# Keys and values of batches 1 to 7 loaded through GpSimd's queue in place of SP's, in a fused kernel of pooled attention and two expert layers

## Chip, cores and metric

One core of a Trainium2 chip. The metric is the device time of one execution in microseconds (us), the median of several runs. All times below are us unless marked ns.

## What is computed

```python
def _attn_ref(q, k, v):                       # (8, 8, 576, 64) each, f32
    k_p = k.reshape(B, H, Sp, pool, D).mean(axis=3)      # pool = 8, Sp = 72
    v_p = v.reshape(B, H, Sp, pool, D).mean(axis=3)
    scores = scale * np.matmul(q, k_p.transpose(0, 1, 3, 2))
    scores = scores - np.max(scores, axis=-1, keepdims=True)
    attn = np.exp(scores)
    attn = attn / (np.sum(attn, axis=-1, keepdims=True) + 1e-09)
    return np.matmul(attn, v_p)
...
x = ...                                       # (4608, 512): the heads side by side
x = g1(x @ w_in) @ w_out                      # 512 -> 2048 -> 512, g1 a clipped square
return g2(x @ w2_in) @ w2_out                 # the same sizes, g2 = relu squared
```

The keys and values of a batch are thus averaged over 8 neighbouring rows before the attention uses them. A batch has 8 heads, and the kernel takes them in pairs: four loads of keys and four of values per batch, `("k", b, p)` and `("v", b, p)` with p = 0 to 3, 64 pairs in all.

## The kernel before

The program is one long row of matmuls on TensorE. The tokens go through in tiles of 128 rows (36 tiles, in blocks of 4), and a loop over steps issues, for each step, the 12 matmuls of the first expert layer's input product (`ph`, L714: hi and lo halves of the operands, three products), one slot of attention work, the 12 matmuls of its output product (`acc`, L775 and L786), and a second slot of attention work. So the attention of a later tile runs between the matmuls of an earlier block. In the last 620 us or so only the second expert layer is left (`cp`, `dp` and their like, L1072 and L1081).

ScalarE (ACT) and VectorE (DVE) work beside it: they split operands into hi and lo (`wihi`/`wilo`, `wohi`/`wolo` at L237 and L241, `gh`/`gl` at L749 and L755), apply the activation (`g`, L747), make the softmax, transpose the attention weights (`aT`, L517, the operand of `px`, L529), and prepare the weights of the second layer (`cb`, L193, out of `z`, L165 to L219). GpSimd (POOL) has few instructions: it clears small pads (L965), and adds integer words for the weights of the second layer (L182); each such add waits for a piece that DVE made (L174), and DVE or ACT go on with its result.

Keys and values come like this. `load_kv` (L292 to L319) takes a buffer of the pool `kvp`, tag `kv`, which has three buffers, and starts the DMA from DRAM. For batches 0 and 1 the pair is laid out over 128 partitions and takes two DMAs (L303, 256 KB, and L313, 32 KB; in batch 0 L309 loads the second part for all pairs at once), and TensorE sums the rows itself (`unit_k` L346, `unit_v` L367), straight out of the loaded buffer. For batches 2 to 7 a load is one DMA of 288 KB over 72 partitions (L317), and `pool_kv` makes the sums on DVE: two adds in place (L332) and a third (L333) that writes `kp` or `vp`. After the third add the buffer is free. `pool_to` (L594 to L600) fixes the order in the program: pair n is summed, and right behind it the load of a later pair is issued. When each pair is due is set by the table `pool_at` (L577).

The program's order is not the engines' order. A scheduler of the tile framework takes the instructions and sets the order on each engine from its own costs, dependencies and buffers. Each engine and each engine's DMA queue then runs strictly in the order set. Before the change SP issues every DMA of the kernel but one or two, 1451 in all: weights, queries, the stores of the attention weights to DRAM and back (`pd<-pad`, L659, and `z<-pd`, L513), results, and the keys and values.

Of the kernel before, what the change touches and what calls it, by code (L numbers as in the profile page):

```python
# [34 lines left out]
def pooled_attention_moe_moe(  # L35
# [11 lines left out]
    nc = tc.nc  # L47
# [244 lines left out]
    def load_kv(nm, b, p):  # L292
        if b == 0 and p == NP - 1:

            a = cv.tile([P, 2, POOL * D], F32, tag="st", name="kv")
        else:
            a = kvp.tile([P if b < ON_PE else SP, 2, POOL * D], F32, tag="kv", name="kv")
        src = k if nm == "k" else v
        kv_t[nm, b, p] = a
        if b < ON_PE:  # L300

            src = src[b, 2 * p:2 * p + 2]
            nc.sync.dma_start(  # L303
                out=a[:, :, 0:BY * D], in_=src[:, 0:BY * P, :].rearrange("h (s r) d -> s h (r d)", r=BY)
            )
            if b == 0:
                if p == (1 if nm == "k" else 0):
                    rest[nm] = gp.tile([S - BY * P, H, D], F32, tag="gh", name="rest")
                    nc.sync.dma_start(  # L309
                        out=rest[nm], in_=(k if nm == "k" else v)[b, :, BY * P:S, :].rearrange("h s d -> s h d")  # L310
                    )
                return
            nc.sync.dma_start(  # L313
                out=a[0:S - BY * P, :, BY * D:(BY + 1) * D], in_=src[:, BY * P:S, :].rearrange("h s d -> s h d")
            )
            return
        nc.sync.dma_start(  # L317
            out=a, in_=src[b, 2 * p:2 * p + 2].rearrange("h (s r) d -> s h (r d)", r=POOL)
        )  # L319

# [235 lines left out]
    for t in range(TB0, NTILE):  # L556
# [12 lines left out]
        if t in first_tile:  # L569
            b = first_tile.index(t)  # L570
# [19 lines left out]
    def load_kv_to(n):  # L590
        while kv_loaded[0] < min(n, len(kv_order)):
            load_kv(*kv_order[kv_loaded[0]])
            kv_loaded[0] += 1
# [604 lines left out]
    for n, u in enumerate(units):  # L1198
        kind, b, i, g = u
# [56 lines left out]
```

## Time and profile before

| | us |
|---|---|
| median of 3 runs | 1620.85 (1620.62 to 1620.98) |
| the profiled execution, its own time | 1620.48 |
| its span in the profile | 1618.7 |
| TensorE (PE) busy | 1612.0 (100%) |
| VectorE (DVE) busy | 1246.5 (77%) |
| ScalarE (ACT) busy | 905.0 (56%) |
| GpSimd (POOL) busy | 54.1 (3%) |
| granted clock of TensorE | 1.00 in every stretch |

How to read it: the span is what the profile sees of the program on the core; the execution's own time is 1.8 longer and is what the runs are compared by. Busy times are sums over instructions; issuing a DMA is not counted as busy. The median stands 0.4 above the profiled execution.

### The profile page before, as it was taken

The numbers are of one execution on the slowest core, as the hardware profiler recorded it, in microseconds if no ns is written. First come the engines' busy times: TensorE is split into PE (matmuls) and PEld (weight loads), VectorE is DVE, ScalarE is ACT, GpSimd is POOL, SyncE is SP. The second block draws the span as 40 slices with busy tenths as digits, with TensorE's granted clock in tenths as the row PEclk, the third lists the DMA queues.
The fourth block names the chain that finished last, engine by engine and source line by source line (L and its number), as shares of the span: only waits on it lengthen the run. The fifth ranks groups of instructions, "written<-read, shape, count | busy, mean of one in ns | idle before, by whom it ended". The sixth has DMA issues, their size and how long they took to land.

```text
span 1618.7 us, 23331 instructions
## 1 busy us (share of the span) xinstructions
PE 1612.0 (100%) x7866; PEld 1317.1 (81%) x7866; DVE 1246.5 (77%) x2231; ACT 905.0 (56%) x1676; POOL 54.1 (3%) x60
## 2 busy tenths in 40 slices
PE   9999999999999999999999999999999999999998
PEld 7678888888878888888888888888888888888887
DVE  6999889898898999998975542578558855975585
ACT  7786566666666666666775532345335533553353
POOL 0000000100000000010100000000000000000000
PEclk9999999999999999999999999999999999999999
DMA  9753344554454554543560474566776776758565
GB/s 257 233 176 99 96 127 151 167 163 120 133 157 147 170 146 132 170 136 134 183 220 7 133 264 148 193 218 207 200 251 220 217 229 210 222 184 252 194 206 142
DMA packets 250279, 283.91 MB, mean 175 GB/s; under 512 B 123440, under 2 KB 155824, under 8 KB 250160
## 3 DMA queue, kind: packets, MB, share of 16 engines
q1 hardware_dynamic: 249072, 282.16, 56.5%
q8 instruction: 63, 1.03, 0.3%
q14 instruction: 56, 0.46, 0.1%
q10 hardware_dynamic: 1088, 0.26, 0.1%
HBM read 217.71 MB, written 64.62 MB: 174 GB/s over the span
## 4 chain that ended last, share of the span: by engine, by line
PE 98%; DMA 1%; DVE 1%; SPq 0%; issue 0%; ACT 0%; DVEq 0%; ACTq 0%
PE ph L714 27%; PE acc L786 26%; PE cp L1072 11%; PE dp L1081 10%; PE dq L1081 5%; PE cr L1072 5%; PE dr L1081 3%; PE cq L1072 3%; PE pss L411 2%; PE px L529 2%; PE acc L775 1%; PE pv L367 0%; DMA kv<-in_v_dram 0%; DMA w<-w2i 0%; PE pk L346 0%; PE dp L1182 0%
## 5 line engine op out<-in xcount | busy, mean ns | idle before, releaser
L714 PE MATMUL ph<-xhi,wihi 128*128 128x512 f32 x576 | 229.9, 399 | 0.0
L1029 ACT ACTIVATE gh<-g 128x512 fp32r<-128x512 f32 x224 | 139.9, 630 | 152.9 <-DVE g L1098 47.9
L714 PE MATMUL ph<-xlo,wihi 128*128 128x512 f32 x576 | 225.0, 391 | 0.0
L714 PE MATMUL ph<-xhi,wilo 128*128 128x512 f32 x576 | 224.9, 390 | 0.0
L786 PE MATMUL acc<-gh,wohi 128*128 128x512 f32 x552 | 222.6, 403 | 0.0
L786 PE MATMUL acc<-gl,wohi 128*128 128x512 f32 x552 | 216.1, 391 | 0.0
L786 PE MATMUL acc<-gh,wolo 128*128 128x512 f32 x552 | 215.5, 390 | 0.0
L821 DVE TENSOR_TENSOR gl<-g,gh 128x512 fp32r<-128x512 f32 x224 | 151.9, 689 | 49.7 <-ACT gh L1029 48.2
L1072 PE MATMUL cp<-x,w 128*128 128x512 f32 x768 | 186.4, 390 | 0.2 <-DMA w<-w2i 0.2
L1072 PEld LDWEIGHTS cp<-x,w 128*128 128x128 f32 x768 | 143.9, 188 | 31.5 <-ACT s L1094 1.4
L237 ACT ACTIVATE wihi<-wi 128x512 fp32r<-128x512 f32 x144 | 90.6, 629 | 123.4 <-PE ph L714 122.7
L1081 PE MATMUL dp<-gh,w 128*128 128x512 f32 x496 | 156.8, 390 | 0.0
L241 DVE TENSOR_TENSOR wilo<-wi,wihi 128x512 fp32r<-128x512 f32 x144 | 101.9, 708 | 46.5 <-ACT wihi L237 43.5
L714 PEld LDWEIGHTS ph<-xhi,wihi 128*128 128x128 f32 x576 | 108.1, 188 | 26.7 <-issue 3.8
L714 PEld LDWEIGHTS ph<-xhi,wilo 128*128 128x128 f32 x576 | 108.2, 188 | 23.1 <-issue 0.2
L714 PEld LDWEIGHTS ph<-xlo,wihi 128*128 128x128 f32 x576 | 108.3, 188 | 21.1 <-issue 0.2
L755 DVE TENSOR_TENSOR gl<-g,gh 128x512 fp32r<-128x512 f32 x154 | 107.0, 695 | 23.1 <-ACT gh L749 20.4
L749 ACT ACTIVATE gh<-g 128x512 fp32r<-128x512 f32 x138 | 86.8, 629 | 64.4 <-DVE g L747 63.5
L1094 ACT ACTIVATE s<-cp 128x512 f32<-128x512 f32 x96 | 57.1, 595 | 116.8 <-PE cp L1072 116.0
L786 PEld LDWEIGHTS acc<-gl,wohi 128*128 128x128 f32 x552 | 103.7, 188 | 22.9
L786 PEld LDWEIGHTS acc<-gh,wohi 128*128 128x128 f32 x552 | 103.8, 188 | 20.9 <-issue 0.6
L786 PEld LDWEIGHTS acc<-gh,wolo 128*128 128x128 f32 x552 | 103.9, 188 | 19.9
(161 smaller groups left out, 2953.3 us busy)
## 6 DMA issues: line engine op xcount, KB each, us to landing
w<-w2i SPq DMA_DIRECT2D x224, 256.0 KB
w<-w2o SPq DMA_DIRECT2D x224, 256.0 KB
w2i<-cb SPq DMA_DIRECT2D x32, 512.0 KB
w2o<-cb SPq DMA_DIRECT2D x32, 512.0 KB
st<-in_moe_w_in_dram SPq DMA_DIRECT2D x30, 512.0 KB
st<-in_moe_w_out_dram SPq DMA_DIRECT2D x30, 512.0 KB
pd<-pad SPq DMA_DIRECT2D x31, 384.0 KB
z<-pd SPq DMA_DIRECT2D x93, 128.0 KB
```

Of the source, the lines that this page charges most:

```text
L237: nc.scalar.activation(out=hi, in_=src, func=AF.Copy)
L241: eng.tensor_tensor(out=lo, in0=src, in1=hi.bitcast(F32), op=ALU.subtract)
L411: nc.tensor.matmul(out=pss[off:off + n, i, :], lhsT=qT[t][:, p, off:off + n], rhs=kbd[b % 2][:, p, :], start=True, stop=True,)
L714: nc.tensor.matmul(out=ph, lhsT=a[:, kk % a.shape[1], :], rhs=c[:, kk, :], start=(i == 0), stop=(i == 3 * KD - 1))
L749: act(out=gh, in_=g, func=AF.Copy)
L755: nc.vector.tensor_tensor(out=gl, in0=g, in1=gh.bitcast(F32), op=ALU.subtract)
L786: nc.tensor.matmul(out=o, lhsT=lhsT, rhs=rhs, start=(f == 0 and x == 0), stop=(f == KF - 1 and x == 2),)
L821: tt(out=out, in0=a, in1=b, op=ALU.subtract)
L1029: act(out=hi, in_=a, func=AF.Copy)
L1072: nc.tensor.matmul(out=out[0], lhsT=w[:, a, k, :], rhs=xq[b, i][c][:, k, :], start=(n == 0 and i in (1, 2, 7)), stop=(n == 5), skip_group_ ...
L1081: nc.tensor.matmul(out=out[d], lhsT=w[:, a, d, :], rhs=x[c], start=(g == 0 and n == 0 and i in (1, 2, 7, 4)), stop=(g == NG - 1 and n == 2 ...
L1094: act(out=snaps[key], in_=a, func=AF.Copy)
```

## The change

`load_kv` gets a variable `queue`, which is SP's queue for batch 0 and GpSimd's for batches 1 to 7, and issues its four DMA calls on it:

```diff
         src = k if nm == "k" else v
+        queue = nc.sync if b == 0 else nc.gpsimd
         kv_t[nm, b, p] = a
         if b < ON_PE:
 
             src = src[b, 2 * p:2 * p + 2]
-            nc.sync.dma_start(
+            queue.dma_start(
                 out=a[:, :, 0:BY * D], in_=src[:, 0:BY * P, :].rearrange("h (s r) d -> s h (r d)", r=BY)
             )
...
-            nc.sync.dma_start(
+            queue.dma_start(
                 out=a[0:S - BY * P, :, BY * D:(BY + 1) * D], in_=src[:, BY * P:S, :].rearrange("h s d -> s h d")
             )
             return
-        nc.sync.dma_start(
+        queue.dma_start(
             out=a, in_=src[b, 2 * p:2 * p + 2].rearrange("h (s r) d -> s h (r d)", r=POOL)
         )
```

64 DMAs move: 16 of batch 1 (eight pairs, two DMAs each) and 48 of batches 2 to 7. SP keeps 1387. From L299 on, every line of the changed kernel has a number higher by one: L303, L313, L317, L332, L333 become L304, L314, L318, L333, L334.

The scheduler answers with another order on several engines. Numbers behind a name count tiles as they are made; `kv_4796` is the same pair before and after.

**GpSimd, the stretch of batches 4 and 5.** Before, its queue holds nothing but the adds of L182 there:

```order
L182 TENSOR_TENSOR z<-st,z 128x512 x2
L182 TENSOR_TENSOR z<-st 128x4x2x32 x4
```

After, the loads stand among these adds, and each waits for a DVE instruction (the one that frees its buffer):

```order
L318 DMA kv_4276<-in_v_dram 72x2x512 [waits DMASW4_49,DVE_49]
L318 DMA kv_4355<-in_k_dram 72x2x512 [waits DMASW5_49,DVE_49]
L318 DMA kv_4664<-in_k_dram 72x2x512 [waits DMASW6_49,DVE_49]
L318 DMA kv_4727<-in_k_dram 72x2x512 [waits DMASW7_49,DVE_49]
L182 TENSOR_TENSOR z_3698<-st_3631,z_3698 128x512 [waits DMAHW1_49,DVE_49,Activation_49]
L182 TENSOR_TENSOR z_3977<-st_3975 128x4x2x32 [waits DVE_49,DMAHW1_49,Activation_49,Pool_49]
L182 TENSOR_TENSOR z_3977<-st_3975 128x4x2x32
L182 TENSOR_TENSOR z_4179<-st_4119 128x4x2x32 [waits DMAHW7_49,DVE_49,Activation_49]
L182 TENSOR_TENSOR z_4179<-st_4119 128x4x2x32
L318 DMA kv_4796<-in_k_dram 72x2x512 [waits DMASW0_49,DVE_49]
L318 DMA kv_4892<-in_v_dram 72x2x512 [waits DMASW1_49,DVE_49]
```

The order of the loads among themselves is that of the program; what is new is that they and the adds of L182 stand in one queue. With three buffers, `kv_4796` takes the buffer that `kv_4355` had.

**VectorE, where the keys of batch 5 are summed.** Before, the stretch from the sum of `kv_4664` to the first add of `kv_4727`:

```order
L333 TENSOR_TENSOR kp_4723<-kv_4664 72x128 [waits DVE_49]
L217 TENSOR_TENSOR s12_4705<-s12_4705,z_4448 128x256 [waits DVE_49]
L241 TENSOR_TENSOR wolo_4620<-wo10_1286,wohi_4619 128x512 [waits Activation_49]
L755 TENSOR_TENSOR gl_4565<-g_4566,gh_4564 128x512 [waits Activation_49]
L218 TENSOR_TENSOR z_4448<-z_4448,z_4636 128x256 [waits DVE_49]
L219 TENSOR_TENSOR z_4448<-z_4448,s12_4705 128x256
L193 TENSOR_TENSOR cb_4775<-s12_4705,cb_4775 128x2x256 [waits Activation_49]
L241 TENSOR_TENSOR wilo_4630<-wi12_1176,wihi_4629 128x512 [waits PE_49,Activation_49]
L332 TENSOR_TENSOR kv_4727<-kv_4727 72x2x256 [waits DMAHW4_49]
```

After, the stretch from the add that frees `kv_4355`'s buffer to the first add of `kv_4796`, which was loaded into that buffer:

```order
L334 TENSOR_TENSOR kp_4660<-kv_4355 72x128 [waits PE_49]
L334 TENSOR_TENSOR kp_4723<-kv_4664 72x128 [waits PE_49]
L748 SCALAR_TENSOR_TENSOR g_4104<-ph_4063,u_4105 128x512 [waits Activation_49]
L193 TENSOR_TENSOR cb_4390<-z_3977,cb_4390 128x2x256 [waits DMAHW3_49,Activation_49]
L334 TENSOR_TENSOR kp_4792<-kv_4727 72x128 [waits PE_49]
L756 TENSOR_TENSOR gl_4103<-g_4104,gh_4102 128x512 [waits Activation_49]
L241 TENSOR_TENSOR wolo_4158<-wo2_675,wohi_4157 128x512 [waits Activation_49]
L333 TENSOR_TENSOR kv_4796<-kv_4796 72x2x256 [waits DMASW3_49]
```

Between the release and the first add that needs the new load stand six instructions. The sums stand earlier in the program than before (their neighbours belong to earlier steps: `g_4104` after, `g_4566` before).

**TensorE, the first expert step after the first block.** The unit of keys of batch 1 whose second pair is `kv_605`. Before:

```order
L346 MATMUL pk_635<-pad1_122,kv_172 64x64 x8
L346 MATMUL pk_635<-pad1_122,kv_172 64x8 x2
L714 MATMUL ph_686<-xhi_415,wihi_570 128x512
L714 MATMUL ph_686<-xlo_416,wihi_570 128x512
L714 MATMUL ph_686<-xhi_415,wilo_571 128x512
L714 MATMUL ph_686<-xhi_415,wihi_570 128x512
L714 MATMUL ph_686<-xlo_416,wihi_570 128x512
L714 MATMUL ph_686<-xhi_415,wilo_571 128x512
L714 MATMUL ph_686<-xhi_415,wihi_570 128x512
L714 MATMUL ph_686<-xlo_416,wihi_570 128x512
L714 MATMUL ph_686<-xhi_415,wilo_571 128x512
```

After:

```order
L715 MATMUL ph_686<-xhi_415,wihi_570 128x512
L715 MATMUL ph_686<-xlo_416,wihi_570 128x512
L715 MATMUL ph_686<-xhi_415,wilo_571 128x512
L715 MATMUL ph_686<-xhi_415,wihi_570 128x512
L715 MATMUL ph_686<-xlo_416,wihi_570 128x512
L715 MATMUL ph_686<-xhi_415,wilo_571 128x512
L715 MATMUL ph_686<-xhi_415,wihi_570 128x512
L347 MATMUL pk_635<-pad1_122,kv_605 64x64 x8
L347 MATMUL pk_635<-pad1_122,kv_605 64x8 x2
```

The keys' matmuls now stand behind seven matmuls of `ph` and not behind eleven. Elsewhere TensorE's order changes in one other place only.

## Rows read from the trace of the kernel before

**Rows 1.** The page, part 1: busy time, share and instructions of each engine.

```profile
PE 1612.0 (100%) x7866; PEld 1317.1 (81%) x7866; DVE 1246.5 (77%) x2231; ACT 905.0 (56%) x1676; POOL 54.1 (3%) x60
```

**Rows 2.** The page, part 4: the chain that ended last, by engine.

```profile
PE 98%; DMA 1%; DVE 1%; SPq 0%; issue 0%; ACT 0%; DVEq 0%; ACTq 0%
```

**Rows 3.** Stretches: busy PE, PEld, DVE, ACT, POOL; clock, DMA share, GB/s.

```profile
40.00:100.00 60.00, 59.90 (x340) 40.27 (x340) 56.19 (x106) 46.81 (x113) 0.26 (x1) 1.00 0.72 213
...
400.00:500.00 100.00, 100.00 (x531) 81.31 (x530) 90.28 (x174) 63.87 (x117) 8.33 (x7) 1.00 0.46 139
```

**Rows 4.** Costliest groups by shape, L332 and L182: busy, mean ns, idle before.

```profile
L332 DVE TENSOR_TENSOR kv<-kv 72x512 f32<-72x512 f32 x48 | 34.8, 726 | 0.0
...
L182 POOL TENSOR_TENSOR z<-st,z 128x512 int32<-128x512 int32 x16 | 26.0, 1626 | 383.4 <-DVE z L174 159.9 <-ACT u L738 60.8 <-ACT u L737 58.3
...
L332 DVE TENSOR_TENSOR kv<-kv 72x256 f32<-72x256 f32 x48 | 19.8, 415 | 0.1
```

**Rows 5.** The timeline of SP's queue, three stretches: start, us, instruction.

```profile
42.32 0.38 SPq L303 DMA_DIRECT2D kv<-in_k_dram  x1
42.75 0.61 SPq L313 DMA_DIRECT2D kv<-in_k_dram  x1
...
166.03 0.34 SPq L659 DMA_DIRECT2D pd<-pad  x1
...
168.46 1.32 SPq L513 DMA_DIRECT2D z<-pd  x3
...
388.81 1.34 SPq L317 DMA_DIRECT2D kv<-in_k_dram  x3
```

**Rows 6.** The timeline of DVE, 405 to 419.

```profile
407.73 0.28 DVE L333 TENSOR_TENSOR kp<-kv 72x128 f32<-72x128 f32 x1
407.93 0.42 DVE L217 TENSOR_TENSOR s<-s,z 128x256 f32<-128x256 f32 x1
408.27 0.68 DVE L241 TENSOR_TENSOR wolo<-wo,wohi 128x512 fp32r<-128x512 f32 x1
408.87 0.68 DVE L755 TENSOR_TENSOR gl<-g,gh 128x512 fp32r<-128x512 f32 x1
...
411.35 0.68 DVE L332 TENSOR_TENSOR kv<-kv 72x512 f32<-72x512 f32 x1
...
418.07 1.23 DVE L517 STREAM_TRANSPOSE aT<-z 96x1024 f32<-96x1024 f32 x1
```

**Rows 7.** The chain of waits followed through 15 to 140: start, us, what.

```profile
43.94 2.74 PE ph L714 x11
...
61.50 1.30 DVE wo L174 x2
63.65 6.36 DMA kv<-in_v_dram
```

**Rows 8.** The chain of waits followed through 0 to 12.

```profile
4.52 4.67 DMA q<-in_q_dram
```

**Rows 9.** The timeline of PE, 41 to 50.

```profile
46.61 0.90 PE L346 MATMUL pk<-pad,kv 128*64 128x64 f32 x20
```

**Rows 10.** The timeline of weight loads, 69 to 71; idle before in brackets.

```profile
69.52 0.20 PEld L367 LDWEIGHTS pv<-kv,pad 64*72 64x72 f32 x2 [0.16 <-DMA kv<-in_v_dram]
70.05 0.86 PEld L367 LDWEIGHTS pv<-kv,pad 128*72 128x72 f32 x8 [0.33 <-DMA kv<-in_v_dram]
```

**Rows 11.** The timeline of PE, 414 to 426.

```profile
415.56 0.40 PE L786 MATMUL acc<-gl,wohi 128*128 128x512 f32 x1
...
423.93 1.09 PE L529 MATMUL px<-aT,vp 72*64 72x128 f32 x16
```

**Rows 12.** What SP's queue waited for: us in total, times, longest.

```profile
SPq L303 <- PE pk L346: 12.1, 2, 11.0
```

**Rows 13.** Costliest groups by shape, L168 and L174.

```profile
L168 DVE TENSOR_SCALAR z<-z 128x512 uint32<-128x512 uint32 x32 | 13.5, 422 | 0.6
...
L174 DVE SCALAR_TENSOR_TENSOR st<-st,z 128x512 uint32<-128x512 uint32 x16 | 11.0, 688 | 0.2
```

More of the change, by code (lines that the diff above doesn't have):

```diff
@@ L316, in load_kv @@
             return
-        nc.sync.dma_start(
+        queue.dma_start(
             out=a, in_=src[b, 2 * p:2 * p + 2].rearrange("h (s r) d -> s h (r d)", r=POOL)
```

## The prediction

> **What bounds the kernel now.** I read the page's busy times first. TensorE is busy for 1612.0 of the span's 1618.7 us [rows 1], so 6.7 us is all that any faster supply could give back, and most of that lies at the program's start and end. The chain that ended last says the same from the other side: 98% of it is TensorE, and 1% each is a DMA and VectorE [rows 2]. Then the stretches: from 100 us on TensorE has no idle time, while DVE is busy for 90.28 of 100 us between 400 and 500 [rows 3]. The reader should see two things there. DVE is the one helper with little to spare, about 9.7 us per 100. And a change of the kernel's time can come only from making TensorE wait, or from a wait that it already has. The groups of L332, 48 adds of either shape, had waited 0.0 and 0.1 us in all [rows 4], so DVE never waited for keys or values. The timelines say why: SP issued three loads at 388.81 [rows 5], and the first add of the second of them ran at 411.35 [rows 6], 22 us later. That lead hides whatever a load takes.
>
> **The change, part by part.** 64 DMAs leave SP's queue. For SP that is 64 issues of some 0.4 us [rows 5], off the path, and for the DMA engines the same bytes.
>
> What costs is the order that comes with it. The loads now stand in one queue with GpSimd's adds, and DVE's sums stand earlier. In the piece of DVE's order shown with the change, six instructions lie between the add that frees a buffer and the first add on what is loaded into it: two of `kp` and four of full size. On DVE's timeline a `kp` takes 0.20 from its start to the next start (407.73 to 407.93) and a full one 0.60 (408.27 to 408.87) [rows 6]: 2 × 0.20 + 4 × 0.60 = **2.8 us of cover**, where before it was 22. I counted the same cover over the whole order for the 45 loads whose buffer DVE frees: 2.8 at six of them (of `kv_3726`, `kv_4276`, `kv_4796`, `kv_6163`, `kv_6696`, `kv_7232`), 2.9, 3.3 and 3.5 at three more, 4.1 at three, 4.5 to 5.1 at seven, and more than that at the others.
>
> Against the cover stands L, the time from a buffer's release to the landing of the load that GpSimd issues into it. The trace of before has no such DMA, so I bound it. From below: a store of 384 KB was issued at 166.03, and its reader's DMAs went out at 168.46, 2.43 later [rows 5]. From above: a load of values, on the chain at 63.65, took 6.36, in a stretch with the DMA engines at a share of 0.72 [rows 7, 3]. Between them, a 256 KB read of queries took 4.67 [rows 8]. A load here reads 288 KB from DRAM, as that one does, but with the DMA share at 0.46 [rows 3] and not in the rush of the start, so somewhat less. GpSimd's part in issuing is not in the trace; SP's issue was 0.34 to 0.61 [rows 5], one GpSimd add 1.63 [rows 4], and I take 1.0 within the total. **L = 4.5**, bounds 2.4 and 6.4.
>
> The Trainium skill, DMA: Bandwidth & Descriptors, section "Anatomy of one DMA — SWDGE (gpsimd) path", gives 2.0 us plus the bytes over 436e3 for one DMA issued from GpSimd; an estimate from that page for 288 KB is 2.7 us, just under the smallest cover, and the sum by it would be about no change. No run here shows such a DMA yet.
>
> Another DVE fact may bear on L. The same 128x512 shape takes 422 ns in L168 and 688 in L174 [rows 13], so some DVE instructions run in a faster mode here. The Trainium skill, SBUF — State Buffer, section "SBUF: two separate sides", says that while DVE runs in such a mode GpSimd cannot write its descriptors. By that rule up to one instruction, 0.4 us, would be added to L where one of them meets an issue; the sum would grow by about 1 us. No row here shows it.
>
> The terms:
>
> 1. *Keys of batch 1 on TensorE.* SP's load of the last pair was issued at 42.32 and 42.75 [rows 5], when its buffer had come free, and TensorE reached it at 46.61 [rows 9] without waiting. Eleven matmuls before it took 2.74, so 0.25 each [rows 7]; it now stands four earlier, at about 45.7. Cover 3.4, two DMAs by GpSimd, the second some 0.2 behind: 4.5 + 0.2 − 3.4 = **+1.3** (0 with L under 3.2; 4.0 with L = 6.4 and 1.0 more for the second issue).
> 2. *Values of batch 1.* TensorE's two waits for a load before 70.05 were 0.16 and 0.33 [rows 10]: SP issued it behind loads that waited for DVE (61.50 to 62.80) [rows 7]. On GpSimd it waits for its buffer only: **−0.5** (0 to −0.5).
> 3. *DVE's waits.* Six at 4.5 − 2.8 = 1.7 are 10.2. Those at 2.9 to 3.5 add 1.6 + 1.2 + 1.0, those at 4.1 three times 0.4: 15.2, and about 12 once loads that stand right behind a wait are counted as partly paid by it. What TensorE feels of it is less. A `gl` that ended at 409.55 was used at 415.56, 6.0 later, and an `aT` that ended at 419.30 was used at 423.93, 4.6 later [rows 6, 11]; one wait of 1.7 is within that, and DVE's 9.7 idle us per 100 win it back in 18 us. Only waits that stand close together reach TensorE. I take a quarter: **+2.8**. The lower bound is 0, if each finds its slack. The upper one is L = 6.4: six at 3.6, three at 3.2, three at 2.3 and seven at 1.6 are 49 us of waits, about all of DVE's idle time from 100 to 700 (58 by the row of 400 to 500), of which I let 20 through.
> 4. *ACT and SP near the seventh tile* (130 us) run in another order, with two splits of weights ahead of the evacuation of a transpose: **+1.0** (0 to 2, the time of three such splits).
>
> Sum: 1.3 − 0.5 + 2.8 + 1.0 = +4.6. Against the profiled execution's 1620.48 that gives 1625.1; the median stands 0.4 above the profiled one, so **1625.4** on the scale of 1620.85. A measurement of this kernel can tell about 0.2% from no change, which is 3.2 us.
>
> **The rivals.**
>
> *A, the forecast:* slower by 3.3 to 11 us, because L is over the smallest covers. Chance 0.44.
>
> *C, landing inside the cover: no change.* The place is the first add after a release; the price is the difference L − 2.8; it decides at L of about 3.3, where six waits of 0.5 vanish in slacks of 4.6 and 6.0, term 1 is near 0, and terms 2 and 4 cancel. Time about 1621. For it speaks the store's 2.43 and that SP's load from 42.75 landed before 46.61, within 3.9 at a DMA share of 0.72. Against it speaks the 4.67 of the queries, and that GpSimd's issue is one more step. It also covers the case that L is 4 and all waits are absorbed. Chance 0.39. The figure of the Trainium skill's DMA: Bandwidth & Descriptors named above points to this rival.
>
> *B, loads held by GpSimd's own order:* slower by over 11. `kv_4796` stands behind five adds of L182 which wait for DVE and ACT themselves; their group waited 159.9 us for DVE before [rows 4]. If an add's input comes after the buffer's release, the load is late by as much, DVE waits for the load, and what GpSimd waits for comes later still. With 2 us more on L, term 3 is at its upper bound: 1620.85 + 20 = about 1640. Against it: the adds' inputs stand ahead of the release in DVE's order at the places I followed. Chance 0.12.
>
> *D, faster:* SP's queue stood 12.1 us waiting for TensorE at L303 [rows 12], with later transfers behind it, and that is gone. The gain is term 2, and at most a little of the 6.7 us that TensorE is idle: 1617 at the best. From 100 us on it has none to give back. Chance 0.05.
>
> **How the numbers follow.** Slower by over 0.2% holds A and B, 0.56; no change C, 0.39; faster D, 0.05. The predicted time is A's, 1625.4. The range takes in C and A, from 1620.4 (term 2 alone) to 1636 (term 3 at more than half of its bound, the others at theirs), and leaves out D, most of B and a corner of A, under 0.2 together. A's own range is 1624.1 to 1632.
>
> **What would show it.** Right: DVE's group of L333 (L332 before) has idle time before it, released by the DMA of `kv`, about 10 us at about a dozen places, each 1 to 2 us, and GpSimd's loads take 4 to 5 us to land; TensorE waits some 1 us at L347 near 46 us, none for `kv` at 70 us, and its busy time stays while its idle time grows by 3 to 5. Wrong: no DMA wait on L333 and the same time (C); or GpSimd's loads issued long after their buffers came free, with its adds of L182 ahead of them waiting, and DVE's waits at 30 us or more (B). The forecast is also wrong in its size if DVE's waits are there at 10 us or more and TensorE does not feel them.

## The result, and the profile after

| | us |
|---|---|
| kernel before, median of 5 runs | 1620.85 (1620.45 to 1623.87) |
| changed kernel, median of 5 runs | 1631.32 (1626.73 to 1631.87) |
| ratio, 95% interval | 1.0056 (1.0040 to 1.0072): slower by 6.5 to 11.7 |
| profiled execution of the changed kernel, and its span | 1631.87, 1630.1 |

The page of the changed kernel, part 1 (busy time of each engine) and the first line of part 4 (the chain that ended last, by engine):

```profile
PE 1616.0 (99%) x7866; PEld 1318.7 (81%) x7866; DVE 1246.3 (76%) x2231; ACT 898.0 (55%) x1676; POOL 96.4 (6%) x124
...
PE 83%; DVE 7%; DMA 4%; ACT 2%; issue 2%; POOL 1%; SPq 0%; DVEq 0%; POOLq 0%; ACTq 0%
```

Against [rows 1, 2]: the work is the same, and the chain that was 98% TensorE now passes through VectorE for 7% and DMAs for 4%. GpSimd's busy time includes issuing its 64 DMAs here; for SP and ScalarE the page leaves issuing out. The stretches of the changed kernel (columns as in [rows 3]) say where TensorE is idle:

```profile
0.00:40.00 40.00, 36.26 (x319) 30.73 (x319) 23.37 (x58) 27.31 (x77) 6.16 (x16) 0.91 0.93 259
40.00:100.00 60.00, 59.03 (x331) 39.12 (x332) 52.94 (x99) 43.13 (x104) 10.21 (x16) 1.00 0.75 211
100.00:200.00 100.00, 98.59 (x512) 80.06 (x511) 96.72 (x193) 68.91 (x151) 11.06 (x14) 1.00 0.49 136
...
300.00:400.00 100.00, 98.14 (x487) 79.56 (x487) 89.17 (x174) 60.70 (x114) 11.93 (x14) 1.00 0.48 144
400.00:500.00 100.00, 99.72 (x504) 80.70 (x503) 88.38 (x171) 63.27 (x118) 12.11 (x12) 1.00 0.47 141
500.00:600.00 100.00, 99.18 (x510) 81.13 (x509) 88.92 (x175) 63.98 (x120) 11.68 (x15) 1.00 0.53 156
```

Three things are in it. From 100 to 600 us TensorE now has gaps of 0.3 to 1.9 us in four of the five stretches of 100 (none from 200 to 300), where before it had none. Between 40 and 100 it lost about a microsecond. And the first 40 us are worse than any GpSimd load can explain: the granted clock is 0.91, and GpSimd's first load goes out at 21.2 us. A finer cut of the start, from 5 to 20 us, and the transpose of the second query tile on TensorE's timeline, changed kernel:

```profile
5.00:10.00 5.00, 2.71 (x46) 1.92 (x45) 0.00 (x0) 1.17 (x3) 0.00 (x0) 1.00 1.05 255
10.00:15.00 5.00, 4.78 (x50) 4.03 (x51) 0.63 (x2) 1.41 (x5) 0.00 (x0) 0.67 0.86 210
15.00:20.00 5.00, 5.00 (x30) 4.97 (x29) 2.83 (x7) 3.53 (x19) 0.00 (x0) 0.65 0.93 270
```

```profile
10.22 0.66 PE L396 MATMUL pq<-ident,q 128*128 128x128 f32 x4 [2.06 <-DMA q<-in_q_dram]
```

and the same matmuls in the kernel before:

```profile
9.23 0.66 PE L395 MATMUL pq<-ident,q 128*128 128x128 f32 x4 [0.62 <-DMA q<-in_q_dram]
```

The tile landed a microsecond later, TensorE was busy for 2.71 of 5 us, and then ran at a granted clock of 0.67 and 0.65: worked out from these two, about two thirds of the ten microseconds at the lower of its two levels (1.2 GHz). By 36 us it was 3.6 late. Whether that belongs to the change is a question for the experiments.

The groups of the first add and of the loads, changed kernel (columns: busy, mean ns, idle before and its releaser), which answer to [rows 4], and the DMA view of the same loads (KB each, median us from issue to landing):

```profile
L333 DVE TENSOR_TENSOR kv<-kv 72x512 f32<-72x512 f32 x48 | 32.5, 681 | 24.4 <-DMA kv<-in_k_dram 17.6 <-DMA kv<-in_v_dram 6.8
...
L318 POOL DMA_DIRECT2D kv<-in_k_dram x24 | 16.7, 695 | 101.8 <-DVE vp L334 48.5 <-DVE kp L334 45.9 <-DVE wi L174 6.9
```

```profile
kv<-in_k_dram POOLq DMA_DIRECT2D x24, 288.0 KB, 5.4
kv<-in_v_dram POOLq DMA_DIRECT2D x24, 288.0 KB, 5.5
```

The wait that was 0.0 is 24.4 us, in 12 places, all of them after 165 us. GpSimd itself waits for DVE's last adds, so a load goes out as soon as its buffer is free: 0.30 us after the third add at most of the 45 loads whose buffer DVE frees, 0.98 at the most. It lands 5.4 to 5.5 us later (median; 3.5 to 9.6 over the 48 loads). What TensorE waited for, changed kernel, four rows of the view of waits (total, times, longest):

```profile
PE ph L715 <- DVE g L748: 1.3, 3, 0.9
...
PE px L530 <- DVE aT L518: 0.6, 1, 0.6
PE px L530 <- DVE pn L437: 0.6, 1, 0.6
PE acc L787 <- DVE wolo L241: 0.3, 1, 0.3
```

These are all the waits that the view lists for TensorE between 162 and 620 us, 2.8 in all, and the kernel before has none there: what makes TensorE wait in that stretch comes through VectorE. One place in full, GpSimd's and then DVE's timeline of the changed kernel:

```profile
295.01 0.69 POOL L318 DMA_DIRECT2D kv<-in_v_dram  x1 [0.44 <-DVE vp L334]
296.45 0.69 POOL L318 DMA_DIRECT2D kv<-in_k_dram  x1 [0.75 <-DVE vp L334]
297.86 0.69 POOL L318 DMA_DIRECT2D kv<-in_k_dram  x1 [0.71 <-DVE vp L334]
303.93 0.69 POOL L318 DMA_DIRECT2D kv<-in_k_dram  x1 [5.38 <-DVE vp L334]
```

```profile
295.87 0.28 DVE L334 TENSOR_TENSOR vp<-kv 72x128 f32<-72x128 f32 x1
296.07 0.68 DVE L756 TENSOR_TENSOR gl<-g,gh 128x512 fp32r<-128x512 f32 x1
296.67 0.68 DVE L241 TENSOR_TENSOR wolo<-wo,wohi 128x512 fp32r<-128x512 f32 x1
297.28 0.28 DVE L334 TENSOR_TENSOR vp<-kv 72x128 f32<-72x128 f32 x1
300.61 0.69 DVE L333 TENSOR_TENSOR kv<-kv 72x512 f32<-72x512 f32 x1 [3.05 <-DMA kv<-in_v_dram]
```

The load of 295.01 had landed at 300.6, 5.6 later; DVE had 2.5 us of work until 297.56 and then stood for 3.05.

### The profile page after: what moved, and what is told of

Its sections match the earlier page's. It is cut to its first block, busy times and chain, and to the rows that moved or that the text cites. A ratio compares the mean times of both kernels' runs of the same rounds, so it can differ in the third digit from the quotient of the medians.

```text
span 1630.1 us, 23406 instructions
## 1 busy us (share of the span) xinstructions
PE 1616.0 (99%) x7866; PEld 1318.7 (81%) x7866; DVE 1246.3 (76%) x2231; ACT 898.0 (55%) x1676; POOL 96.4 (6%) x124
## 4 chain that ended last, share of the span: by engine, by line
PE 83%; DVE 7%; DMA 4%; ACT 2%; issue 2%; POOL 1%; SPq 0%; DVEq 0%; POOLq 0%; ACTq 0%
PE ph L715 21%; PE acc L787 20%; PE cp L1073 11%; PE dp L1082 10%; PE dq L1082 5%; PE cr L1073 5%; PE cq L1073 3%; PE dr L1082 3%; PE pss L412 2%; PE px L530 2%; DMA kv<-in_k_dram 1%; DMA st<-in_moe_w_in_dram 1%; DMA q<-in_q_dram 1%; DMA st<-in_moe_w_out_dram 1%; DVE wilo L241 1%
```

## The experiments

Theory **cover**: the cost is that DVE reaches a load's first add before the load has landed. Rivals: the change spoils the **start**; GpSimd's loads slow **other work** by contention or by its queue; the **new order** of weights and their staging costs on its own. In the table, "late" is by how much a matmul of `ph` starts later than the same matmul in the profile of before: the first one that the kernel before starts after 36.6, 162 and 560 us. A difference between two columns is what a stretch cost, free of what the start did. Each row is one execution.

| profiled execution | late at 36 | at 162 | at 560 | 162 to 560 | DVE's wait for kv |
|---|---|---|---|---|---|
| the change | 3.64 | 6.56 | 11.21 | 4.65 | 24.4 |
| e1, again | 2.37 | 5.04 | 12.10 | 7.06 | 27.1 |
| e2, batch 1 only | 2.17 | 3.26 | 3.26 | 0.00 | 0.0 |
| e3, batches 2 to 7 only | 4.81 | 11.01 | 16.45 | 5.44 | 26.8 |
| e4, adds held | 0.47 | 5.62 | 6.03 | 0.41 | 2.5 |
| e5, SP's queue, adds held | 4.63 | 4.44 | 4.44 | 0.00 | 0.0 |
| e6, split loads | 2.57 | 3.74 | 5.89 | 2.15 | 18.7 |
| e7, ScalarE's queue | 7.17 | 11.27 | 12.85 | 1.58 | 10.8 |
| e8, SP's queue, q1 early | −0.90 | −1.05 | −1.05 | 0.00 | 0.0 |
| e9, change, q1 early | −0.88 | 1.18 | 5.39 | 4.21 | 25.8 |
| e10, split, q1 early | −0.72 | 1.11 | 2.47 | 1.36 | 19.5 |
| e11, delayed, q1 early | −0.99 | −0.46 | 5.48 | 5.94 | 28.0 |
| e12, adds held, q1 early | −0.77 | 6.16 | 6.26 | 0.10 | 2.6 |

**e1: the changed kernel again.** No edit.

> The changed kernel once more. In the profiled execution of the result TensorE was 3.6 us late at 40 us already, with the granted clock at 0.65 to 0.67 from 10 to 20 us, before GpSimd had issued a load (its first went out at 21.2). Theory 'cover' (the cost is that VectorE reaches a load's first add before the load has landed): the late start is chance, so some executions should come out near 1627 us (clock 1.000) and others near 1631 (0.998), and the kernel before has such executions too. Rival 'start' (the change itself spoils the start): all executions near 1631 with a clock of 0.998, and none of the kernel before.

Measured: 1633.03 (1631.13 to 1635.60), the kernel before on the same chip 1623.06 (1620.67 to 1626.97), ratio 1.0068 (1.0055 to 1.0081). The executions of the kernel before spread over 6 us on this chip, with clocks down to 0.996, and the late start needs no load of GpSimd: e3, whose first goes out at 67 us, and e5, which has none, were late by 4.81 and 4.63 at 36 us. But the two groups near 1627 and 1631 did not show: all five executions lie above 1631, and the time after 162 us varies by itself, 4.65 and 7.06 in two executions of one kernel.

**e2 and e3: the two halves of the change.**

```diff
-        queue = nc.sync if b == 0 else nc.gpsimd
+        queue = nc.gpsimd if b == 1 else nc.sync      # e2
+        queue = nc.gpsimd if b > 1 else nc.sync       # e3
```

> GpSimd's queue for batch 1 alone, SP's for all others. Theory 'cover': VectorE's adds go back to leads of 13 us and more, no wait of VectorE for keys or values; what is left is TensorE's wait for the last pair of keys near 46 us (3 us of waiting, some 1 us net in the changed kernel) and the new order near the seventh tile (about 1 us): 1622 to 1624.5. Rival 'start': 3.6 us more than that, about 1626 to 1628, with a clock of 0.998.

Measured: 1623.89, ratio 1.0005 (0.9995 to 1.0015). No wait of DVE for keys or values, nothing lost after 162 us, 1.1 between 36 and 162.

> GpSimd's queue for batches 2 to 7 alone. Theory 'cover': VectorE waits for keys and values as in the changed kernel (24 us in 12 places), and from 150 us on TensorE loses what it lost there (4 us); the first 150 us are as before: 1623.5 to 1626.5. Rival 'batch 1 carries most of it': under 1623. Rival 'start': 1627 or more with a clock of 0.998, as loads of GpSimd are there at all.

Measured: 1633.97, ratio 1.0070 (1.0053 to 1.0088): 7.5 us above the top of what was expected, and in the profiled execution 4.81 of it is a late start. After 162 us it loses 5.4, as the change does. But it loses 6.2 from 36 to 162, and nearly half of that is one wait of TensorE (its timeline):

```profile
77.48 2.08 PE L368 MATMUL pv<-kv,pad 128*72 128x128 f32 x10 [2.71 <-DMA kv<-in_v_dram]
```

SP issued that load at 68.47, in step with the late start (63.65 before [rows 7]), but with GpSimd's load of 67.45 just ahead of it, it took 9.0 us to be in, where it had taken 6.36. In the change, where this load is GpSimd's too and goes out earlier, TensorE does not wait for it; so the halves don't add up.

**e4 and e5: the order of DVE's adds.** The adds may not be put ahead of the DVE instruction written just before them; with GpSimd's loads (e4) and with SP's (e5).

```diff
+        last = next(i for i in reversed(nc.cur_bb.bb.instructions) if i.engine == mybir.EngineType.DVE)
+        with tc.issue_after(last):
-        for w in (4 * D, 2 * D):
+            for w in (4 * D, 2 * D):
...
```

> The change as it is, but VectorE's three adds of each pair may not be put ahead of the VectorE instruction written just before them (an order on the same engine, no wait). By the order the cover between the release of a buffer and the first add on its next load is then 2.9 us once, 4.6 to 5.7 four times, and 7.5 or more at the other 40 loads, where it was 2.8 to 5.1 at nineteen. Theory 'cover': VectorE's waits for keys and values fall from 24 us to under 6, and what is left is batch 1: 1622 to 1625. Rival 'queue' (loads of GpSimd slow other work down, by contention or by its own adds behind them): no better than the changed kernel with the same start, 1627 to 1631.

Measured: 1629.90, ratio 1.0047 (1.0033 to 1.0060). The rival for the total, the theory for its place: DVE's wait falls from 24 to 2.5 us, and with it the loss after 162 us from 4.65 and 7.06 to 0.41. GpSimd still issues every load. But 5.2 us were lost between 36 and 162, more than in the change (2.9 and 2.7), so the loss that left one stretch came back in another.

> The kernel before, all loads on SP's queue, with VectorE's adds held behind the VectorE instruction written before them, as in the run before. It tells whether the 5 us that TensorE lost between 38 and 165 us with GpSimd's loads and held adds come from the holding or from GpSimd's loads. Theory: by the order the smallest cover is 12 us, so no wait of VectorE for keys or values, and no loss: 0 to +1 us against the kernel before. Rival: holding the adds of batch 2 delays the pieces that ScalarE and the weight loads wait for: +2.5 to +4, lost between 100 and 145 us.

Measured: 1621.60, ratio 1.0001 (0.9992 to 1.0010). Holding the adds costs nothing by itself; late by 4.63 at 36 us, it stayed so. What e4 loses before 162 us comes with GpSimd's loads, or with the order that they bring.

**e6: two DMAs for each load.**

```diff
-        queue.dma_start(
-            out=a, in_=src[b, 2 * p:2 * p + 2].rearrange("h (s r) d -> s h (r d)", r=POOL)
-        )
+        for h in range(2):
+            queue.dma_start(
+                out=a[:, h], in_=src[b, 2 * p + h].rearrange("(s r) d -> s (r d)", r=POOL)
+            )
```

> The change, with each load of batches 2 to 7 made by two DMAs of one head (144 KB each) in place of one of 288 KB. GpSimd spent 0.69 us on issuing one, so the second half goes out 0.69 later, and the first add needs both; the order keeps its pattern of covers. Theory 'cover': VectorE's waits for keys and values grow by about 0.7 us in some 13 places, from 24 to 27 us to 33 to 37, and TensorE feels a quarter of it or more: 12 to 14 us over the kernel before on the same chip, where the changed kernel stood at 10. Rival: the wait is the transfer's own time, and two halves are no slower than one: waits and time as in the changed kernel.

Measured: 1625.97 against 1621.16, ratio 1.0021 (1.0009 to 1.0032): the opposite of what was expected. The second half does go out later, but the pair lands sooner: a half took 4.2 (keys) and 4.6 (values) to land, both were in 5.1 after the first was issued (median), where the whole took 5.5, and DVE's wait fell to 18.7. So the lever worked, and I had its sign wrong.

**e7: ScalarE's queue.** `queue = nc.sync if b == 0 else nc.scalar`.

> The loads of batches 1 to 7 on ScalarE's queue in place of GpSimd's. Theory 'cover': what costs is that a load is issued when its buffer comes free, with little work of VectorE ahead of its first add (2.8 us at four loads, 3.7 to 5.6 at seven, in this order), and it does so on any queue: VectorE waits 5 to 15 us for keys and values, and ScalarE now waits for VectorE's adds as well, 3 to 8 us over the kernel before. Rival 'GpSimd': the loss belongs to GpSimd's way of issuing: no more than 1.5 over the kernel before.

Measured: 1629.55, ratio 1.0046 (1.0032 to 1.0060), 8.4 us over the kernel before and just beyond the 3 to 8 expected. As the theory has it, DVE waits here too, 10.8 us, with no load on GpSimd's queue, and 1.6 are lost after 162. The rest of what the profiled execution lost came earlier: it was late by 7.17 at 36 us already (TensorE had waited 2.12 for the second query tile, and the granted clock was 0.62 and 0.70 from 10 to 20 us), and it lost 4.1 more up to 162. There TensorE's longest waits are for ScalarE (2.0 for `pn`, 1.0 for `aT`, 0.8 for `gh`). That ScalarE is late because it issues the loads was not shown.

**e8: the start, in the kernel before.** One DMA is issued two places earlier; no other instruction moves.

```diff
     load_kv_to(2)
-    load_q_to(0)
+    load_q_to(1)
     load_kv_to(NP)
```

> The kernel before, with one DMA moved: the load of the second query tile goes out ahead of the third and fourth pair of keys of batch 0, where it stood behind them. TensorE's wait for that tile was 0.6 us in the profile of before and 1.4 to 2.1 in three others, and in those the granted clock then fell to about 0.65 for some us. Theory 'start': wait and low clock both go, and with them most of the spread between executions: 1.5 to 3 us faster than the kernel before on this chip, and no execution above 1622. Rival: the spread has another cause, and the time is the same within 0.5 us.

Measured: 1619.36 (1619.01 to 1621.20) against 1621.16 (1620.13 to 1628.45), ratio 0.9984 (0.9975 to 0.9993). The wait is gone, and the finer cut of the start shows no fall of the clock:

```profile
8.23 0.71 PE L395 MATMUL pq<-ident,q 128*128 128x128 f32 x5
```

```profile
5.00:10.00 5.00, 5.00 (x62) 3.71 (x61) 0.00 (x0) 1.65 (x4) 0.00 (x0) 1.00 1.23 271
10.00:15.00 5.00, 5.00 (x61) 4.48 (x61) 3.17 (x9) 3.62 (x18) 0.00 (x0) 1.00 1.10 261
```

As expected: 1.8 us faster, and no execution above 1622. Its executions spread over 2.2 us where those of before spread over 8.3. This version beats both kernels, and it is the ground on which the change can be weighed without the start.

**e9: the change on that ground.** The edit of e8 in the changed kernel.

> The change together with the early second query tile, which took the spread out of the start (1619.4 for the kernel before with it): so the cost of the change by itself. By the traces TensorE lost 2.8 to 3.0 us between 38 and 165 us and 4.4 to 6.8 from 165 to 550. Theory 'cover': 1626.5 to 1629.5, spread under 2 us, clock 1.000. Rival: the change also spoils the start by itself, then 1631 or more.

Measured: 1627.62 (1626.81 to 1630.93), ratio to the kernel before 1.0036 (1.0024 to 1.0049). The time is as expected; the executions spread over 4.1 us and not under 2. With e8's 0.9984 the change by itself costs 1.0036 / 0.9984 = 1.0052, or 8.4 us (about 6 to 11 with the intervals of both): in the profiled execution 2.1 between 36 and 162 us, and 4.2 from there to 560. By name and shape of the instructions, the orders of VectorE, ScalarE and TensorE are those of the changed kernel. On this chip, that of e1, the early query tile took 5.4 us off the changed kernel (from 1633.03), on the chip of e8 1.8 off the kernel before; so the late start may weigh more in the changed kernel, and why was not tried.

**e10: e9 with the split loads of e6.**

> As the last, with each load of batches 2 to 7 in two DMAs of one head. The order of VectorE's instructions between release and first add is the same as in the last run at all 45 loads; only the time to land differs (the halves landed 4.2 and 4.6 us after issue, 0.53 apart, the whole 5.4). Theory 'cover': 3 to 5 us over 1619.4, 1622.5 to 1624.5, and VectorE's waits near 19 us. Rival: the gain of the split loads was chance or came from the start: as the last run.

Measured: 1623.35 (1620.57 to 1625.21), ratio 1.0008 (0.9999 to 1.0016): as expected, and 4 us above e8, where the change stands 8; none of its 11 executions is as slow as the fastest of e9's five. The order between release and first add is the same at all loads, the stretch to 162 us costs much the same (1.8), and after it 1.4 in place of 4.2. The place shown above, here on GpSimd's and DVE's timelines:

```profile
289.24 1.04 POOL L319 DMA_DIRECT2D kv<-in_v_dram  x2 [0.44 <-DVE vp L335]
```

```profile
294.03 0.69 DVE L334 TENSOR_TENSOR kv<-kv 72x512 f32<-72x512 f32 x1 [2.24 <-DMA kv<-in_v_dram]
```

and the same place in e9:

```profile
289.79 0.70 POOL L318 DMA_DIRECT2D kv<-in_v_dram  x1 [0.45 <-DVE vp L334]
```

```profile
295.40 0.69 DVE L333 TENSOR_TENSOR kv<-kv 72x512 f32<-72x512 f32 x1 [3.07 <-DMA kv<-in_v_dram]
```

From the first issue to the first add 4.8, in e9 5.6. Over all the loads the landing comes 0.6 us sooner (median 5.0 after the first issue, in e9 5.6); that took 6.3 us off DVE's waits and 2.9 off what TensorE lost from 162 to 560.

**e11: e9 with the loads delayed.** GpSimd clears half of the buffer first; the load overwrites it.

```diff
+        nc.gpsimd.memset(a[:, 0, :], 0.0)
         queue.dma_start(
             out=a, in_=src[b, 2 * p:2 * p + 2].rearrange("h (s r) d -> s h (r d)", r=POOL)
```

> As the run before the last (whole loads), with GpSimd clearing the first head of each buffer of batches 2 to 7 (72x512) before it issues the load into it: the load then overwrites it, so nothing changes but that a load goes out some 0.5 to 0.7 us after its buffer's release, and the DMA's bytes and number stay. The fewest VectorE instructions between release and first add stay at six (four loads in place of seven, three more at seven). Theory 'cover': VectorE's waits grow to 29 to 36 us and the time to 10 to 13 over 1619.4, 1629.5 to 1632.5. Rival: what counts is the DMA's shape or its contention, not when it lands: as without the clearing.

Measured: 1625.90 (1623.78 to 1627.10), ratio 1.0021 (1.0011 to 1.0030): below e9 and far below what was expected. What DVE waited for, in the view of waits (total, times, longest):

```profile
DVE kv L334 <- DMA kv<-in_k_dram: 21.9, 7, 6.2
...
DVE kv L334 <- DMA kv<-in_v_dram: 6.1, 3, 2.4
```

28.0 us, only 2.2 more than e9. This kernel's order is not e9's: four loads have the smallest cover in place of seven, and between 36 and 162 us it lost 0.5 where e9 lost 2.1. After 162 it lost 5.9 against 4.2, the way the theory says but not the amount. So the delay did not make a clean dose, and it supports the theory only in that stretch.

**e12: e9 with the adds held.**

> The change with VectorE's adds held, and the early second query tile. Theory 'cover': VectorE's waits under 6 us, nothing lost from 165 us on; what TensorE loses before 165 us stays, 5 us in the trace of the run with held adds: 1623.5 to 1625.5. Rival: the loss from 165 us on does not come from VectorE's waits: no better than the change without the holding.

Measured: 1626.90 (1626.40 to 1629.03), ratio 1.0032 (1.0020 to 1.0045), above the 1623.5 to 1625.5 expected and little better than e9. After 162 us it loses 0.1: that half of the expectation is as clear as it can be. But it loses 6.9 between 36 and 162, where 5 was expected. There TensorE waits for the attention pieces, and ScalarE, which makes them, waits for the staged weights of the first layer (ScalarE's timeline, three of its waits):

```profile
70.99 0.67 ACT L160 ACTIVATE wo<-st 128x512 f32<-128x512 f32 x1 [2.02 <-DMA st<-in_moe_w_out_dram]
...
96.95 0.67 ACT L160 ACTIVATE wo<-st 128x512 f32<-128x512 f32 x1 [2.29 <-DMA st<-in_moe_w_out_dram]
...
117.73 0.67 ACT L160 ACTIVATE wo<-st 128x512 f32<-128x512 f32 x1 [2.82 <-DMA st<-in_moe_w_out_dram]
```

In the kernel before, ScalarE never waits for the DMA of `wo`, and 2.3 us in all for that of `wi`; here `wo` alone is 10.2, in e9 6.2 with 4.2 for `wi`. This second loss, 2 to 3 us in the change, is shown by place and by what waited. Its cause, SP's new order of staging loads and queries or contention with GpSimd's loads, was not tried apart and stays open. The traces of the profiled executions hold a hint of each. In the changed kernel the staging loads issued from 66 to 81 us took 5.1 to 10.3 us to land, those of the rest of the stretch to 162 us 3.3 to 6.7; the one of 66.78 took 9.1, and its counterpart of 62.87 in the kernel before was used at 68.35 without a wait, so 5.5 at the most. But in e11 the staging loads issued from 65 to 74 us took 7.2 to 8.5, and it lost only 0.5 there.

## Why the prediction was right, and where its sum was off

The direction, the mechanism and the range held: 1631.32 lies in 1620.4 to 1636, and the forecast case (over the smallest covers, no more) is the one that happened. The predicted 1625.4 was 6 us short. Part of what was measured is not in the sum at all: the late start, and most of ScalarE's waits for staged weights. That the total still lies in the forecast case's own range of 1624.1 to 1632 owes something to its width.

- **What bounds the kernel.** Right in the main: TensorE's idle time grew from 6.7 to 14.1 us, by 7.4 where 3 to 5 was forecast. But its busy time grew too, by 4.0, which the sum left out; the low clock from 10 to 20 us accounts for some 3.4 of it (an estimate: ten microseconds at 0.66).
- **L, 4.5 of 2.4 to 6.4.** Too low. It was to be the time from a buffer's release to the landing: measured 5.7 (median of 45 loads), 0.3 until the load goes out and 5.5 until it is in, 5.9 at the place shown. The issue itself was 0.69, not 1.0. I had taken the 256 KB read of 4.67 [rows 8] and gone down for the lighter traffic; the loads of 288 KB took longer with the DMA share at about 0.48 than that read at the start. Nor is L one number: in five of six groups of three loads issued within 3 us the first landed 4.6 to 6.0 after its issue and the third 6.1 to 9.3. The fastest of the 48 loads took 3.5, so all of them are over the smallest cover of 2.8, and the rival without a change (C) falls with it. The fit of the Trainium skill, DMA: Bandwidth & Descriptors, section "Anatomy of one DMA — SWDGE (gpsimd) path", gave 2.7 as an estimate, under the fastest of these loads and half of the median; here the measurement decides.
- **Term 1 (keys of batch 1), +1.3.** Measured +0.2 in the change (late by 3.64 at 36 us, by 3.80 at 52). TensorE's wait was there, on its weight loads:

```profile
49.45 0.55 PEld L347 LDWEIGHTS pk<-pad,kv 128*64 128x64 f32 x16 [0.49 <-DMA kv<-in_k_dram]
```

  The load had gone out at 46.22 and its first part was in after 3.2, under the L that I took for it.
- **Term 2 (values of batch 1), −0.5.** The two waits of [rows 10] are gone, but nothing shows as gained: from 52 to 100 us the changed kernel lost 0.9 more.
- **Term 3 (DVE's waits), 12 us of waits and +2.8.** This is the term that was mis-sized. The places were a dozen, as said, but 24.4 to 27.1 us of waits in place of 12, of which 4.2 to 7.1 reached TensorE. The share that I guessed, a quarter, was about right (0.16 to 0.26); the waits were twice as long. L alone accounts for that: with 5.7 in place of 4.5 the same sum gives 36 us, and 28 with the allowance that made 12 out of 15.2.
- **Term 4 (ScalarE and SP near the seventh tile), +1.0.** The place was there but is part of a larger loss, 2.1 to 2.9 us between 36 and 162 us, with ScalarE waiting for staged weights, the most of it from 71 to 84 us. I had read SP's queue only for what left it, not for how the rest of it was put in a new order.
- **The start.** 3.6 us of the profiled execution's loss came before GpSimd's loads could matter: up to 20 us all engines and SP's queue run the same instructions in the same order as before, and the tile that TensorE waited for is needed at 10. The row that warned of it was the chain at 4.52 [rows 8], the only DMA that TensorE waited for at all in the first 12 us; I used it as a bound and did not ask what the kernel's own spread came from.
- **The rivals.** B (loads held behind GpSimd's adds) did not happen: all 45 loads whose buffer DVE frees went out within 1.0 us of the release. D (faster) fell: SP's relief gave nothing back. GpSimd's issue of a load took 0.69 at nearly all loads, 1.04 at the most, beside a DVE that is 87 to 97% busy from 100 to 600 us. What the Trainium skill, SBUF — State Buffer, section "SBUF: two separate sides", says of GpSimd's descriptors would be a part of L here, and no run tells it apart.

The proof that term 3 is a wait for landings, and not GpSimd as such, is the table: with GpSimd issuing all loads and DVE's adds moved away from the releases the loss from 162 to 560 us is 0.1 to 0.4 (e4, e12); with the order kept and the landing 0.6 sooner it is a third (e10 against e9). One execution of the changed order differs from another by up to 2.9 there (4.2 to 7.1 in three of them); these three lie clearly below all of them. What is shown in this way is about half of the 8 us; the 2 to 3 us before 162 have their place, but not their cause.

## What to carry to other kernels

Moving DMAs to another queue changed the scheduler's order on every engine here. Read in the new order, load by load, how much work lies between the instruction that frees a buffer and the first that needs the next load in it, and hold that against the longest landing that the trace shows for the size, not the middling one. A load that was issued 20 us early cost nothing on SP's busy queue; one issued at the moment of release on a nearly idle queue had to be waited for wherever the work ahead of its first use was shorter than its landing. And before weighing an edit of half a per cent, look at what the kernel's own spread is made of: here the place of one load among the first seven was worth 1.8 us, or 0.16%, of the kernel before.

## What the runs showed that I had not expected

- In the seven executions in which TensorE waited 1.4 to 2.1 us for one load near 9 us, a lower granted clock followed (0.67 and 0.65 from 10 to 20 us in the changed kernel, 0.50 there in e3), and TensorE was 2 to 5 us late at 36 us (the change, e1, e2, e3, e5, e6), in e7 7. With waits of 1.09 (e4), 0.62 (the profile of before) and less (e8 to e12) the clock stayed at 1.00 there.
- On GpSimd's queue two DMAs of 144 KB landed sooner than one of 288 KB: 4.2 and 4.6 after issue, 0.52 apart, the pair 5.1 after the first issue, against 5.5, and 4.8 against 5.6 from the first issue to the first add at the same place of the program.
- GpSimd's issue of a load is short and even: 0.69 for 288 KB, 0.53 for 144 KB.
